# The opening of a fused attention and gated-FFN block: constants ahead of x, statistics of one row pair on ScalarE, packed K norms, and a score bound added by products for the first two score groups

## The chip, the cores and the metric

The kernel runs on one core of a Trainium2 chip. The core has TensorE (PE in the profile, with PEld for its weight loads), VectorE (DVE), ScalarE (ACT), GpSimd (POOL), SyncE (SP) and 16 DMA engines. SP issues nearly all DMAs here. Each engine takes its instructions in the order in which the program gives them; instructions of different engines wait for each other through semaphores. The metric is the device time of one execution in microseconds. The kernel before took 963.77 us as the median of 3 runs (963.26 to 965.14).

## What is computed

One pre-norm transformer block on 2048 rows of 512 values (bf16), with 32 heads of 16 and a hidden width of 1792, without masks, biases or learnt norm weights.

```python
x = A_x
h = x + _A_ref(_layernorm(x, axis=-1), A_wqkv, A_wo)
h2 = h + _B_ref(_layernorm(h, axis=-1), B_w_gate, B_w_up, B_w_down)
# _A_ref: qkv = x @ wqkv; p = softmax(q k^T * Dh**-0.5); o = p v; o @ wo
# _B_ref: (sigmoid(x w_gate) * (x w_up)) @ w_down
```

The softmax runs over all 2048 keys, so 32 x 2048 x 2048 exponentials are taken. B_x is not used.

## The kernel before

**The exponential sets the shape.** Scores are made transposed: a tile is 128 keys by 512 queries of one head. Three such tiles make a group (`groups`, GU = 3), one group is one step, and there are 683 steps. `emit_scores` (L764) issues a step: three products of K (`KT`) with Q (`QB`) into one of two PSUM buffers of three banks (`pss2`, L767), and one ScalarE exponential over 128 x 1536 (L794). In every fourth step from step 8 on, and in some more later (`split`), ScalarE takes two of the three tiles and VectorE the third, in five instructions spread over four steps: L813 from PSUM, L816 and L819 one step on, L822 two steps on and L826 three steps on.

**The softmax bound.** In place of a row maximum the kernel subtracts a bound, the product of the norm of q with the largest norm of a key, and the subtraction is part of the score product. K and Q rows stand at the even partitions of `KT` and `QB`. The odd partitions of `KT` hold 1.0, and those of `QB` hold zero, but for one in each half of 64, which holds the bound. `emit_q_rows` (L215) loads Q into `QB` by four DMAs, `emit_q_bound` (L226) the bound by two; for step 0 the second of these goes out from ScalarE's queue. The bound of a query is `y0` (a root by bit arithmetic of its squared norm, `q_root`) times `nks` (from the largest squared key norm, `k_bound`, L179), rounded into `bnd` (`q_bound`, L203).

**Prologue (L238 to L390), up to step 0.** Eight loads of two row tiles each bring x on SP's queue (L80), three loads the K, Q and V parts of `wqkv` on ScalarE's queue (L82). GpSimd makes the identity and fills `QB[0]`, `KT[:,1]` and the ones column of `Vaug`; VectorE clears `ones_blk`, `km2`, `quad`, fills `KT[:,0]` and clears `acc`. For a pair u of row tiles, `stats` takes two BN_STATS (L139) and two BN_AGGREGATE (L140) and adds the epsilon (L144) on VectorE, then GpSimd raises to the power -0.5 (L146); `apply` (L150) normalises on VectorE; `trans` transposes on TensorE (L273) and copies on ScalarE (L278). The order is stats of pair u+1, then apply of pair u. Between them come K of head block 0 in four chunks of 512 rows (`k_chunk`, L288, the last by halves), Q of chunk 0, seven V tiles (`v_tile`, L160 and L212), and for each K chunk a norm product over all 128 columns of `ones_blk` (`norm`, L169) and a maximum (`k_max`, L173). `k_bound` and the bound close it. The small constants `head_of` and `ones_blk` are finished behind `stats(0)` (L320, L323). `gate` (L388) is a GpSimd copy that waits for `bnd`; behind it GpSimd clears `QB[1]`, makes `same` (L958), fills `KT[:,2]` to `KT[:,7]` (L433), clears `wo_pad` (L954) and copies `ident_f`.

The prologue has six one-bank PSUM tiles in turn (`pm_tile`), which become the two score buffers; besides there are one bank for `acc` and one for `ps_misc`, which the later fills use (`pmh["pool"]`).

**Steps.** In step i the program emits the scores, then the products with V that are due (`emit_pv`, L857, into `acc`, by `plan_pv`, three key tiles of a head group per four steps), then due callbacks (`later`), then filler products (`emit_fill`, at the rate of `rate(i)`, L755). The filler is one long generator (L742): V tiles 7 to 15 (`fill_v`, L408), K and Q of the other head blocks (`fill_k`, L422, with the fills of `KT` on GpSimd at L433), Q of the later chunks, then for each finished chunk the output projection and the FFN. When a head group of four ends, `emit_norm` (L834) copies `acc` to `xs_all` (L838), sends the sums through DRAM (`sd`), takes the reciprocal five steps later (L849), sends it through DRAM again (`rd`) to `rb_all`, and scales ten steps later (L845). `QB` of the next head group is loaded at key tile 12 of the present one in chunks of 512 queries, and at key tile pair 0 in the two last chunks of 256.

Of the kernel before, what the change touches and what calls it, by code (L numbers as in the profile page):

```python
# [10 lines left out]
FP32 = mybir.dt.float32  # L11
BF16 = mybir.dt.bfloat16
# [6 lines left out]
def kernel(  # L19
# [30 lines left out]
    GM = 188  # L50
    G1 = 680
    QS = DH ** -0.5 * 1.4426950408889634 * 2.0 ** 23
    LEAD = 0.106445681
    PA, PB, PC = 0.70747575 / LEAD, 1.37730748 / LEAD, 1.77561468 / LEAD
    ONE_BITS = (127.0 + math.log2(LEAD)) * 2.0 ** 23
# [23 lines left out]
    for i in range(8):  # L79
        nc.sync.dma_start(out=xb[:, 2 * i:2 * i + 2, :], in_=x_v[:, 2 * i:2 * i + 2, :])  # L80
    for part in (1, 0, 2):
        nc.scalar.dma_start(out=wqkv_sb[:, :, part * D:(part + 1) * D],  # L82
                            in_=wqkv_v[:, :, part * D:(part + 1) * D])
# [24 lines left out]
    nks = const.tile([P, 1], FP32)  # L108
    bnd = const.tile([P, QC], BF16)
# [62 lines left out]
    def k_max(ps, n):  # L172
        nc.vector.tensor_reduce(out=km2[:, n:n + 1], in_=ps[:], axis=AX.X, op=ALU.max)  # L173
# [5 lines left out]
    def k_bound():  # L179
        m2 = small.tile([P, 1], FP32, name="m2")  # L180
        nc.vector.tensor_reduce(out=m2[:], in_=km2[:], axis=AX.X, op=ALU.max)
        z0 = small.tile([P, 1], mybir.dt.int32, name="z0")
        sqrt_bits(z0[:], m2[:])
        z = z0[:].bitcast(FP32)
        ri = small.tile([P, 1], FP32, name="ri")
        nc.vector.reciprocal(out=ri[:], in_=z)
        tq = small.tile([P, 1], FP32, name="tq")
        nc.vector.scalar_tensor_tensor(out=tq[:], in0=ri[:], scalar=m2[:, 0:1], in1=z,
                                       op0=ALU.mult, op1=ALU.add)
        nc.vector.tensor_scalar(out=nks[:], in0=tq[:], scalar1=-0.5175, scalar2=None, op0=ALU.mult)  # L190
# [45 lines left out]
    NV0 = 7  # L236

    def prologue(pro):  # L238
        warm = pro.tile([P, 8], FP32, name="warm")
        nc.vector.memset(warm[:], 0.0)  # L240
        nc.scalar.activation(out=warm[:], in_=warm[:], func=ACT.Exp)
        make_identity(nc, ident_bf[:])
        nc.gpsimd.memset(pw_neg[:], -0.5)
        nc.gpsimd.memset(QB[0][:], 0.0)
        nc.gpsimd.memset(KT[:, 1, :], 1.0)
        nc.gpsimd.memset(Vaug[:, :, :, DH:DH + 1], 1.0)
# [5 lines left out]
        nc.vector.memset(KT[:, 0, :], 1.0)  # L252
        nc.vector.memset(acc[:], 0.0)

        mvs, rss, xns, pts, sqs, pns = {}, {}, {}, {}, {}, {}
        ku = stages[0]

        def stats(u):
            mvs[u] = pro.tile([P, 2, nc.vector.BN_AGGR_DIM], FP32, name="mvs", bufs=3)
            for i in range(2):  # L260
                ln_stats(xb[:, 2 * u + i, :], mvs[u][:, i, :])
            rss[u] = ln_rstd(mvs[u], 2)

        def apply(u):
            xns[u] = pro.tile([P, 2, D], BF16, name="xn2", bufs=3)
            for i in range(2):
                ln_apply(xns[u][:, i, :], xb[:, 2 * u + i, :], mvs[u][:, i, :], rss[u][:, i:i + 1])

        def trans_mm(u):
# [5 lines left out]

        def trans(u):
            trans_mm(u)
            nc.scalar.copy(out=xnT[:, :, 2 * u * P:(2 * u + 2) * P], in_=pts[u])  # L278

        def square(key, ps, scale=1.0):  # L280
            sqs[key] = pro.tile([P, QC], BF16, name="sq", bufs=3)
            nc.scalar.activation(out=sqs[key][:], in_=ps[:], func=ACT.Square, scale=scale)

        def norm(key):
            pns[key] = pm_tile()
            norm_mm(pns[key], 0, sqs[key][:])

        def k_chunk(n):  # L288
            ps = pm_tile()
            for c in range(DC):  # L290
                qk_mm(ps, 1, 0, n, c)
            cols = slice(n * QC, (n + 1) * QC)
            nc.scalar.copy(out=ku[:, cols], in_=ps[:])
            square(n, ps)
            k_spread(ku, 0, cols, nc.sync)

        def k_half(ps, u):
            hc = slice(QC // 2 * (u % 2), QC // 2 * (u % 2 + 1))
            for c in range(DC):
                nc.tensor.matmul(ps[:, hc], lhsT=wqkv_sb[:, c, D:D + P], rhs=xnT[:, c, u * QC // 2:(u + 1) * QC // 2],  # L300
                                 start=(c == 0), stop=(c == DC - 1))

        def q_chunk():
# [4 lines left out]
            square("q", ps, QS)  # L308
            ready.add(("q", 0, 0))
            emit_q_rows(0)  # L310

        def v_tile(t, copy=nc.scalar.copy):
            ps = pm_tile()
            for c in range(DC):
                v_mm(ps, t, c)
            v_store(t, ps, copy)
            ready.add(("v", t))

        def consts():
            nc.vector.tensor_reduce(out=head_of[:], in_=ident_bf[:].rearrange("p (h r) -> p h r", r=DH),  # L320
                                    axis=AX.X, op=ALU.max)
            for b in range(4):
                nc.vector.tensor_copy(out=ones_blk[:, b, :, 8 * b:8 * b + 8],  # L323
                                      in_=head_of[:].unsqueeze(1).to_broadcast([P, 4, 8]))

        def ln_step(u):
            if u + 1 < NT // 2:
                stats(u + 1)
            apply(u)

        stats(0)
        consts()
        ln_step(0)
        trans(0)
        ln_step(1)
        trans(1)
        v_tile(0)
        ln_step(2)
        trans(2)
        k_chunk(0)  # L340
        ln_step(3)
        trans(3)
        q_chunk()
        norm(0)
        ln_step(4)
        trans(4)
        k_chunk(1)
        norm("q")
        ln_step(5)
        trans(5)  # L350
        v_tile(1)
        v_tile(2)
        norm(1)
        ln_step(6)
        trans(6)
        ps2 = pm_tile()
# [655 lines left out]
```

## Time and profile before

| | before |
|---|---|
| median of 3 runs | 963.77 us (963.26 to 965.14) |
| time of the profiled execution | 962.96 us |
| its span, first to last instruction | 961.1 us |
| TensorE, VectorE, ScalarE, GpSimd busy | 826.7, 788.1, 895.3, 41.5 us |
| first exponential starts | 34.24 us |
| last exponential (step 682) starts | 929.73 us |
| DMA moved | 28.38 MB |

Times in a profile count from the first instruction of the profiled execution, in us; a mean duration is in ns. A row of the instruction groups gives line, engine, operation, tile written and tiles read, the shapes and how often it ran, then busy time and mean duration, then the engine's idle time in front of it and who ended most of it. The chain of waits is followed back from the last instruction: a row gives start, length and what the chain spent it on; "DMA" there is from issue to landing, "issue" is time in which the engine waited for nothing that the profile shows.

### The profile page before, as it was taken

How to read it: one execution, taken by the hardware profiler on the slowest of the kernel's cores; microseconds unless marked ns; L12 is line 12 of the kernel's file. 1: busy time of each engine (PE TensorE's matmuls, PEld its weight loads, DVE VectorE, ACT ScalarE, POOL GpSimd, SP SyncE). 2: the span in 40 equal slices, each digit the busy share in tenths (PEclk: the TensorE clock that was granted, in tenths of full speed). 3: DMA queues.
4: the chain of work that ended last, by engine and by line, in shares of the span. 5: the costliest groups of instructions: out<-in, count | busy, mean ns of one | idle time of the engine just before them, and what ended most of it. 6: DMA issues, size and time to landing. Idle time of an engine off the chain costs nothing.

```text
span 961.1 us, 17150 instructions
## 1 busy us (share of the span) xinstructions
PE 826.7 (86%) x6327; PEld 337.8 (35%) x6425; DVE 788.1 (82%) x1428; ACT 895.3 (93%) x767; POOL 41.5 (4%) x49
## 2 busy tenths in 40 slices
PE   4887888888788999988788999988788999888998
PEld 2322222222222332222222233222355555455646
DVE  8589998888788888899888888888888788777653
ACT  4789999999999999999999999999998999899872
POOL 4700000000000000000000000000000000000000
PEclk9999999999999999999999999999999999999999
DMA  5001350000013000000011000001011000110010
GB/s 160 21 8 50 114 117 17 16 16 2 16 26 103 16 16 17 19 12 26 14 27 26 16 16 15 14 15 26 16 31 23 16 13 13 27 32 16 9 35 12
DMA packets 37500, 28.38 MB, mean 30 GB/s; under 512 B 17708, under 2 KB 32776, under 8 KB 37416
## 3 DMA queue, kind: packets, MB, share of 16 engines
q1 hardware_dynamic: 35828, 25.71, 10.4%
q10 hardware_dynamic: 1588, 1.58, 0.5%
q8 instruction: 50, 0.82, 0.4%
q14 instruction: 34, 0.28, 0.1%
HBM read 20.31 MB, written 2.61 MB: 24 GB/s over the span
## 4 chain that ended last, share of the span: by engine, by line
PE 40%; DVE 26%; ACT 23%; issue 7%; DMA 3%; SPq 1%; ACTq 0%; DVEq 0%; POOL 0%; POOLq 0%
PE pss L783 20%; ACT pt L794 12%; PE acc L864 8%; PE pm L530 6%; ACT stg L794 4%; ACT wd L794 4%; DVE stg L813 3%; ACT QTu L794 2%; PE pm L546 2%; DVE reg L816 2%; DVE st L139 2%; DVE pt L826 2%; DVE y L822 2%; PE pm L506 2%; DVE reg L543 1%
## 5 line engine op out<-in xcount | busy, mean ns | idle before, releaser
L783 PE MATMUL pss<-QB,KT 64*128 64x512 bf16 (+3 forms) x2542 | 475.8, 336 | 86.9 <-ACT pt L794 43.8
L794 ACT ACTIVATE pt<-pss 128x1536 bf16<-128x1536 f32 (+1 forms) x392 | 501.1, 1363 | 16.3 <-PE pss L783 12.0
L783 PEld LDWEIGHTS <-KT 64*128 64x128 bf16 (+1 forms) x2560 | 181.4, 95 | 345.3 <-issue 232.5
L794 ACT ACTIVATE stg<-pss 128x1536 bf16<-128x1536 f32 (+1 forms) x140 | 183.1, 1355 | 4.6 <-PE pss L783 3.8
L813 DVE TENSOR_SCALAR stg<-pss 128x512 int32<-128x512 f32 x123 | 84.8, 689 | 69.3 <-PE pss L783 53.0
L864 PE MATMUL acc<-pt,Vaug 128*17 128x512 bf16 (+1 forms) x1471 | 112.5, 338 | 4.5 <-DVE xs_all L838 3.2
L794 ACT ACTIVATE wd<-pss 128x1536 bf16<-128x1536 f32 (+1 forms) x80 | 103.8, 1390 | 2.7 <-PE pss L783 2.4
L794 ACT ACTIVATE QTu<-pss 128x1024 bf16<-128x1024 f32 (+1 forms) x71 | 95.5, 1345 | 1.7 <-PE pss L783 1.2
L819 DVE SCALAR_TENSOR_TENSOR y<-reg 128x512 f32<-128x512 f32 x123 | 85.2, 692 | 4.2
L822 DVE SCALAR_TENSOR_TENSOR y<-y,reg 128x512 f32<-128x512 f32 x123 | 84.2, 684 | 1.1
L864 PEld LDWEIGHTS <-Vaug 128*17 128x17 bf16 x2560 | 50.4, 89 | 96.1 <-issue 80.8
L530 PE MATMUL pm<-reg,reg 128*128 128x512 bf16 (+1 forms) x252 | 55.6, 333 | 8.7 <-DVE reg L543 6.6
L530 PE MATMUL pm<-reg,wu 128*128 128x512 bf16 (+1 forms) x280 | 58.1, 338 | 1.5 <-ACT sg L535 1.2
L546 PE MATMUL pm<-wd,reg 128*128 128x512 bf16 x173 | 51.2, 381 | 5.7 <-issue 2.9
L146 POOL TENSOR_TENSOR rs<-ve,pw_neg 128x1 f32<-128x1 f32 (+1 forms) x24 | 17.7, 736 | 888.9 <-DVE ve L144 758.0
L816 DVE TENSOR_SCALAR reg<-stg 128x512 int32<-128x512 int32 x123 | 52.0, 423 | 2.0
L864 PE MATMUL acc<-stg,Vaug 128*17 128x256 bf16 (+1 forms) x564 | 50.6, 326 | 0.6 <-DVE stg L826 0.4
L543 DVE SCALAR_TENSOR_TENSOR reg<-sg,pm 128x512 bf16<-128x512 f32 x56 | 38.2, 682 | 13.9 <-PE pm L530 13.5
L826 DVE SCALAR_TENSOR_TENSOR pt<-y,stg 128x512 bf16<-128x512 f32 x70 | 47.8, 683 | 1.8
L535 ACT ACTIVATE sg<-pm 128x512 f32<-128x512 f32 x56 | 35.6, 637 | 10.1 <-PE pm L530 9.8
L813 DVE TENSOR_SCALAR wd<-pss 128x512 int32<-128x512 f32 x45 | 30.9, 688 | 15.9 <-PE pss L783 14.9
L165 PE MATMUL pm<-reg 128*128 128x512 bf16 x112 | 35.6, 391 | 2.2 <-issue 0.8
(129 smaller groups left out, 707.5 us busy)
## 6 DMA issues: line engine op xcount, KB each, us to landing
rb_all<-rd SPq DMA_DIRECT2D x96, 64.0 KB
reg<-in_A_x_dram SPq DMA_DIRECT2D x8, 256.0 KB
xr<-in_A_x_dram SPq DMA_DIRECT2D x16, 128.0 KB
out_dram<-ob SPq DMA_DIRECT2D x15, 128.0 KB
rb_all<-rd SPq DMA_DIRECT2D x60, 32.0 KB
KT<-stg SPq DMA_DIRECT2D x7, 256.0 KB
reg<-in_B_w_gate_dram SPq DMA_DIRECT2D x4, 448.0 KB
wu<-in_B_w_up_dram SPq DMA_DIRECT2D x4, 448.0 KB
```

Of the source, the lines that this page charges most:

```text
L165: nc.tensor.matmul(ps[:], lhsT=wqkv_sb[:, c, w0:w0 + P], rhs=xnT[:, c, n * QC:(n + 1) * QC], start=(c == 0), stop=(c == DC - 1))
L530: nc.tensor.matmul(ps[:, i * w:(i + 1) * w], lhsT=wt[:, c, f * P:(f + 1) * P], rhs=hnT[:, c, 0:w], start=(c == 0), stop=(c == DC - 1))
L543: nc.vector.scalar_tensor_tensor(out=out, in0=a, scalar=1.0, in1=b, op0=ALU.add, op1=ALU.mult)
L546: nc.tensor.matmul(ps[:], lhsT=hT[:, f, tt * P:(tt + 1) * P], rhs=wd[:, f, :], start=(f == 0), stop=(f == FC - 1))
L783: nc.tensor.matmul(pss[:, ui, h * w:(h + 1) * w], lhsT=KT[rows, g, kt * P:(kt + 1) * P], rhs=QB[n_qg % 2][rows, j, 0:w], start=True, stop= ...
L794: ex = nc.scalar.activation(out=pt[:, 0:na, :], in_=pss[:, 0:na, :], func=ACT.Exp, scale=DH ** -0.5 / QS)
L813: return nc.vector.tensor_scalar(out=e_bits, in0=src, scalar1=ONE_BITS, scalar2=0.0, op0=ALU.add, op1=ALU.max)
L816: nc.vector.tensor_scalar(out=e_man, in0=e_bits, scalar1=0x7FFFFF, scalar2=-0x40800000, op0=ALU.bitwise_and, op1=ALU.bitwise_or)
L819: nc.vector.scalar_tensor_tensor(out=e_pol, in0=m, scalar=PA, in1=m, op0=ALU.add, op1=ALU.mult)
L822: nc.vector.scalar_tensor_tensor(out=e_pol, in0=e_pol, scalar=PB, in1=e_man.bitcast(FP32), op0=ALU.add, op1=ALU.mult)
L826: nc.vector.scalar_tensor_tensor(out=dst, in0=e_pol, scalar=PC, in1=e_bits.bitcast(FP32), op0=ALU.add, op1=ALU.mult)
L864: nc.tensor.matmul(acc[32 * j:32 * j + VW, 0:w], lhsT=Vaug[:, kt, 4 * g + j, :], rhs=p[:, h * w:(h + 1) * w], start=(kt == 0), stop=(kt == ...
```

## The change

**Loads.** The first x pair is split: row tile 0 on SP's queue, row tile 1 on ScalarE's. The `wqkv` parts move to SP's queue behind x.

**Constants.** `head_of` and `ones_blk` are made before x arrives; `same` and the ones column of `Vaug` are made on ScalarE; the clear of `acc` moves to the fills. Fills of `KT` and `QB` on GpSimd go over the same bytes as half as many 4-byte elements (two bf16 ones in one word). `gate` now waits for `ones_blk`, and stands in front of the fill of `KT[:,0]` and the clear of `QB[1]`; nothing holds GpSimd behind the last statistics.

**Statistics.** The epsilon add moves from VectorE to GpSimd. Pair 1's mean and variance come from ScalarE: two Identity passes with a sum, two Square passes with a bias and a sum. `stats` runs two pairs ahead of `apply`.

**Norms.** K chunks 0 to 2 put their norms into 32 rows each of one PSUM tile, with one maximum over 96 rows, spread by a small product; chunk 3 goes by halves of 256. `k_bound` drops a Newton step (three of five small instructions) and a slack factor of 1.0735 takes its place; for block 0 the bound comes straight from `z0`.

**First two groups.** `QB[1]` gets a copy of the first Q rows without a bound. Steps 0 and 1 multiply over all 128 rows of it, and add the bound by a second product into the same bank, of a broadcast identity column with `bnd`.

**V.** Three V tiles instead of seven stand ahead of step 0's exponential (the third between the two products of step 0); tiles 3 to 6 go to the filler, 3 and 5 of them through `acc`.

**Steady part.** Next `QB` load at key tile 2 instead of 12 from head group 6 on (`EARLY`); reciprocal and scaling two steps later except for the last head group or two of a chunk (`wait`); where a head group's first key tile is due, the filler comes before the product with V (`early_fill`).

The diff, cut to its core:

```diff
-    for i in range(8):
+    nc.sync.dma_start(out=xb[:, 0, :], in_=x_v[:, 0, :])
+    nc.scalar.dma_start(out=xb[:, 1, :], in_=x_v[:, 1, :])
+    for i in range(1, 8):
         nc.sync.dma_start(out=xb[:, 2 * i:2 * i + 2, :], in_=x_v[:, 2 * i:2 * i + 2, :])
     for part in (1, 0, 2):
-        nc.scalar.dma_start(out=wqkv_sb[:, :, part * D:(part + 1) * D],
+        nc.sync.dma_start(out=wqkv_sb[:, :, part * D:(part + 1) * D],
...
+    def k_fold(kd, n, col):
+        pc = ps_misc.tile([P, 512], FP32, name="pm")
+        nc.tensor.matmul(pc[:, 0:4], lhsT=same[0:n].rearrange("p r h -> p (r h)"), rhs=kd[0:n, :],
+                         start=True, stop=True)
+        k_max(pc[:, 0:4], km2[:, col:col + 1])
...
-    NV0 = 7
+    NV0 = 3
+    OB = 2
+    def fill_ones(eng, ap):
+        eng.memset(ap.bitcast(FP32), TWO_ONES)
...
+        gate = pro.tile([P, 1], BF16, name="gate")
+        nc.gpsimd.tensor_copy(out=gate[:], in_=ones_blk[:, 3, 3, 31:32])
+        fill_ones(nc.gpsimd, KT[:, 0, :])
+        clear(QB[1][:])
...
+        x_sums = sums_act(1)
         stats(0)
-        consts()
-        ln_step(0)
+        stats_act(1, x_sums)
+        stats(2)
+        apply(0)
         trans(0)
-        ln_step(1)
+        stats(3)
+        clear(QB[0][:, 0:2, :])
+        apply(1)
         trans(1)
-        v_tile(0)
-        ln_step(2)
+        apply(2)
         trans(2)
         k_chunk(0)
...
+        v0 = v_prod(0, pm_tile())
+        v_cast(0, v0)
+        stats(7)
+        nc.gpsimd.memset(bnd[:].bitcast(FP32), 0.0)
+        apply(6)
+        norm_part_of(1)
         trans(6)
...
+        q_root(acc, 0)
+        apply(7)
+        v1 = v_prod(1, pm_tile())
+        norm_part_of(2)
+        km4 = small.tile([P, 1], FP32, name="km4")
+        k_max(pnp[0:96, :], km4)
...
+        kd = k_spots(km4, 96)
         ps3 = pm_tile()
         k_half(ps3, 6)
         k_half(ps3, 7)
+        pn3 = pm_tile()
+        norm_half(pn3, 6)
+        k_max(pn3[:, 0:QC // 2], km2[:, 1:2])
+        k_fold(kd, 96, 0)
+        v_cast(1, v1)
+        k_copy(2, ps2)
+        k_copy(3, ps3)
+        pn3 = ps_misc.tile([P, 512], FP32, name="pm")
+        norm_half(pn3, 7)
+        k_max(pn3[:, 0:QC // 2], km2[:, 2:3])
+        m2 = k_most()
+        sqrt_bits(z0[:], m2[:])
+        nc.vector.tensor_scalar(out=bnd[0:32, :], in0=y0[0:32, :].bitcast(FP32), scalar1=z0[0:32, :].bitcast(FP32),
+                                scalar2=-SQRT_SLACK, op0=ALU.mult, op1=ALU.mult)
...
+        emit_q_bound(0)
         k_spread(ku, 1, slice(0, S), nc.sync)
-        gate = pro.tile([32, 1], BF16, name="gate")
-        nc.gpsimd.tensor_copy(out=gate[:], in_=bnd[0:32, 0:1])
-        nc.gpsimd.memset(QB[1][:], 0.0)
...
-            rates = (4.0 if i > 5 else 0.0, 4.0 if i < 6 else 2.0 if i > 16 else 0.0, 0.0, 4.0)
+            rates = (4.0, 4.0 if i < 6 else 2.0 if i > 16 else 0.0, 4.0 if i < 6 else 0.0, 4.0)
...
-        pss = pss2[(i + 1) % 2]
+        pss = pss2[i % 2]
...
+        if i < OB:
+            for ui, (c, g, k, j) in enumerate(group):
+                nc.tensor.matmul(pss[:, ui, :], lhsT=KT[:, g, k * P:(k + 1) * P], rhs=QB[1][:, j, :],
+                                 start=True, stop=False)
+            if i == 0:
+                v_cast(2, v_prod(2, pm_tile()))
+            for ui, (c, g, k, j) in enumerate(group):
+                nc.tensor.matmul(pss[:, ui, :], lhsT=ident_bf[:, j:j + 1].to_broadcast([P, P]), rhs=bnd[:],
+                                 start=False, stop=True)
+            parts = []
...
-            if k == (12 if per_bank(c) == 1 else 0) and j == 3 and n_qg + 1 < len(qgs):
+            if k == (0 if per_bank(c) > 1 else 2 if n_qg in EARLY else 12) and j == 3 and n_qg + 1 < len(qgs):
...
+        wait = 2 if g < NG - 1 - (c == NC - 1) else 0
...
-            later(i + 10, scale)
-        later(i + 5, recip)
+            later(i + 10 + wait, scale)
+        later(i + 5 + wait, recip)
...
+            early_fill = i >= 2 * CYC and any(u[2] == 0 for u in us)
+            for u in us:
+                if early_fill and u[2] == 0:
+                    emit_fill(i)
                 emit_pv(*u[:3], i)
```

## The prediction

> **What bounds it now.** I read the shares first, then ScalarE's busy time by stages, then the chain of waits of the first 60 us, then the rows around ScalarE's later pauses. By the shares ScalarE does most:
>
> ```profile
> PE 826.7 (86%) x6327; PEld 337.8 (35%) x6425; DVE 788.1 (82%) x1428; ACT 895.3 (93%) x767; POOL 41.5 (4%) x49
> ...
> 34.24:100.00 65.76, 61.06 (x49) 1.00 0.09 23
> 100.00:200.00 100.00, 99.86 (x82) 1.00 0.25 63
> ...
> 600.00:700.00 100.00, 97.18 (x82) 1.00 0.07 17
> 700.00:800.00 100.00, 96.46 (x85) 1.00 0.09 21
> 800.00:900.00 100.00, 92.73 (x80) 1.00 0.09 22
> ```
>
> The columns after the stage are its length, ScalarE's busy time, the clock and the DMA. From the first exponential on ScalarE is the bound, so time comes from two places: exponentials that start earlier, and ScalarE's pauses, 4.7 us before 100 and some 15 us behind 300. The way to the first exponential, from the chain of waits (start, length, what):
>
> ```profile
> 0.74 3.74 DMA reg<-in_A_x_dram
> ...
> 9.96 0.61 DVE st L139
> 10.58 0.02 issue
> 10.60 0.18 DVE mvs L140
> 10.79 0.59 DVE st L139
> 11.37 0.02 issue
> 11.40 0.19 DVE mvs L140
> 11.59 0.02 issue
> 11.61 0.17 DVE ve L144
> 11.78 0.64 DVE xn L150 x2
> ...
> 30.82 0.48 DVE bnd L203
> ...
> 31.37 1.99 DMA QB<-bnd
> 33.36 0.12 issue
> 33.48 0.60 PE pss L783 x3
> ```
>
> VectorE holds the chain from 4.50 to 25.74: 2.46 us a pair (9.96 to 12.42), of which 1.62 are statistics, 0.19 the epsilon, 0.65 the normalising. Then come transposes, the last K chunk, norms, maxima and bound to 31.30, 2 us of DMA, and the first exponential at 34.24.
>
> **The prologue, step by step.** *Start.* x's first landing, at 4.48, shares the DMA engines with the weights; split and with the weights behind it I take 3.5 (bounds 3.0 and 4.48). The constants (0.73 for `head_of`, 0.41 for four copies) then end at about 2.8, ahead of x; today they lie on the chain. *VectorE* takes seven statistics of 1.62, eight normalisings of 0.65 and `q_root` at 0.60: 3.5 + 11.3 + 5.2 + 0.6, and 0.2 of waiting for GpSimd in front of the first normalising, 20.9 at the end of `apply(7)` against 25.74. *ScalarE* gains four passes of about 0.6 (as a 512-wide Square, 0.62; sums out of an instruction are in no row, 0 to 0.3 each), 0.6 for V's ones and 1.1 for `same`; it stood idle for 6.88 us ahead of its first copy. Pair 1's root is ready at 8.3, wanted at 9.2: if the cover goes, each 0.3 costs its own length. *GpSimd* gets the epsilon adds, 0.2 each beside 0.73 for a root; statistics run two pairs ahead, which hides both. *Weights* behind x: 2.6 MB of x and K at the 263 GB/s of the first 10 us land at about 11 to 12; K's first product needs them at 11.8; 0 to 0.2. On SP's queue three weight issues and four more `QB` issues (0.5 to 0.6 each, 22.6 at the latest today) stand ahead of K copies that nothing needs before step 3: nothing.
>
> Here VectorE is no longer last; **TensorE and ScalarE are**. After `apply(6)` at 19.6 come the transposes, K chunk 2 and V tile 1 (0.86 each), norm product and transposes to 22.7 on TensorE; VectorE's maximum waits for the norm (22.4 to 23.0) and the copy behind it ends at 23.4; K's last half 24.1, its Square 24.5, its norm product behind the fold (free at 24.7) 25.0, maximum 25.5, two small ones 25.8, bound 26.3. V tile 2 stands ahead of the bound's products (three at 0.22 and 0.16 to drain), so these end at 27.4, and so starts the first exponential. If TensorE's pace (0.427 us a 512-wide product until 17.3, 0.216 after) changes at 12.5 or at 18 instead of my 14.7, it is 27.0 or 28.5. *Bound rows by DMA* are now wanted by step 2: today they are there 2.1 us after the bound, now both go through SP behind two K copies, one issue (0.70) later, about 3.6 behind the bound, and step 2 wants its exponential 3.8 behind it with 0.7 of products ahead of that: 0.5 late at worst, 0.3 taken. 0.3 more for hand-overs that I left out: **28.0 in effect, 6.2 earlier**.
>
> **A queue that opens: GpSimd.** Today `gate` holds eight fills (six of `KT`, two of `wo_pad`, 1.745 us apart) until 31.36. After the change nothing does: behind the last root, at 20.2, they run in one piece, six at half the elements, 0.87 (by bytes 1.75), and two at 1.745, to 29.0. What they do to VectorE the trace shows twice. The epsilon add at 6.24 took 0.81 instead of 0.17, to the end of a fill; and in the rows of VectorE (start, length, engine, line, operation):
>
> ```profile
> 46.60 2.25 DVE L816 TENSOR_SCALAR reg<-wd 128x512 int32<-128x512 int32 x1
> ...
> 53.42 0.42 DVE L816 TENSOR_SCALAR reg<-wd 128x512 int32<-128x512 int32 x1
> ```
>
> The long one ran to the end of the last fill, past one boundary between two. So a scaling of 4-byte words in SBUF waits; `bnd` (4-byte in, 0.47) is one, and `apply` (bf16, 0.406) may be. For `apply` the rows speak against it: beside it GpSimd's roots keep 0.72 to 0.79. For `bnd` it costs nothing to a boundary's wait of 0.3 (27.7), or 2.9 if it waits to 29.0; I take the short one.
>
> The Trainium skill, SBUF — State Buffer, section Who interferes with whom, says that VectorE in a two-port mode and GpSimd take a shared port pair as an exclusive lock, and that copies and scalings in SBUF, bf16 ones too, can take it. By that `apply(7)` would wait as well, the third rival below; the trace agrees for 4-byte words (2.25 against 0.42) and not for `apply` beside the roots (0.72 to 0.79).
>
> **The first steps.** V tiles 3 to 6 come after the first exponential now: 0.86 of TensorE and 0.69 of VectorE each. In steps 1 to 5 a step with a V tile takes TensorE 0.6 + 0.86 = 1.47 against 1.34 of exponential; five such steps lag 0.65, and 0.74 is in hand. Later steps hold as many filler products as before, other ones. I take +0.4 (to +2.0 if two tiles show in full). Against it the 2.25 of L816, which is on the chain and ends in a ScalarE pause of 1.78 at 53.41, goes: the fills are over 9 us before. -1.7, together **-1.3**. Half as many bound instructions on VectorE, the other fills and the swapped score buffers: nothing, beside ScalarE's 99%.
>
> **The steady part.** The delayed reciprocal meets the one pause that is plainly its own (chain, start, length):
>
> ```profile
> 829.95 3.23 DMA s_all<-sd
> 833.19 0.02 issue
> 833.21 0.20 DVE r_all L849
> ```
>
> VectorE waited there, its next FFN output came late, TensorE waited 1.78 and ScalarE 1.95. Two steps, 2.7 us, cover it. The other three such waits (535, 746, 877) lie beside ScalarE's work or cost under 0.8. The filler ahead of a new head group covers only one product (0.2 to 0.3) of TensorE's waits for `xs_all` (0.95 at 645 and 728). Earlier `QB` loads are six issues moved on SP; no product behind step 2 waits for `QB` today, so they gain nothing but can meet another DMA. I take **-1.9** (bounds -4, with the pauses of 1.0 at 647 and 1.3 at 730, and +1, if the shifted transfers meet others).
>
> **Sum.** -6.2 - 1.3 - 1.9 = -9.4. The profiled execution took 962.96 (its span 961.1 and 1.9 around it), so 953.6; the median of the runs lies 0.8 above it, so 954.4.
>
> **Rivals**, each in the median's terms.
> - *The bound waits for the last fill.* For: L816 let one boundary pass. Against: that was 0.1 us behind its issue. 29.0 + 0.5 + 0.8 of products gives 30.3, 2.9 later than 27.4, less 0.3 as step 2's rows are then no later: 957.0. Chance 0.24.
> - *The V tiles eat it.* Steps 9 to 29 already pause for 4.7 us, so two tiles show in full and steady changes give nothing: -6.2 + 1.5 + 0 = -4.7: 959.0. Chance 0.14.
> - *`apply(7)` waits for the fills too.* Then it ends at 29.7 and the rest of its chain, 5 us, gives 34.7: +0.5 - 1.3 - 1.9: 961.1. Chance 0.11.
> - *Slower: the same wait, with long fills.* If a fill of 4-byte words goes by bytes, 1.75, six of them end at 35.0 and the first exponential starts at 40.7: +6.5 - 3.2: 967.1. It decides from 1.56 us a fill on. Against: the small fills go by elements (128 in 0.205, 2048 in 1.8). Chance 0.05.
>
> The forecast has 0.46; its own range, from the bounds above, is 950.5 to 960. About 0.2% is what a measurement of this kernel can tell from no change; of the third rival, which lies across that line, half counts as the same. Faster 0.89, same 0.06, slower 0.05. The range 950.5 to 960.5 leaves out the last two rivals.
>
> **What would show it.** First exponential near 28; `apply(7)` ending near 21; GpSimd's fills ending near 29 at 0.87 each; `bnd` at about 0.5 and not 2 or more; L816 at 0.42 throughout; no pause of 1 us or more in steps 9 to 29 or near step 617. It is wrong if `apply` or `bnd` shows microseconds, if step 2 waits for `QB` by over 0.6, or if pauses behind step 300 add to more than today's 15 us.

## The result, and the profile after

The changed kernel took 973.84 us (median of 4 runs, 973.56 to 976.31), the kernel before 964.45 in the same comparison: ratio 1.0103, 95% interval 1.0081 to 1.0126. It is 9.4 us slower where 9.4 us faster was forecast. The profiled execution took 976.31 (span 974.5); it is the slowest of the four, while the profiled execution of before (962.96) lies below its four. So the two profiles lie 13.4 apart where the medians lie 9.4 apart, and the places below add to more than the loss of the medians. From the page of the profile after:

```profile
PE 839.3 (86%) x6334; PEld 339.5 (35%) x6433; DVE 786.2 (81%) x1410; ACT 900.3 (92%) x779; POOL 34.6 (4%) x57
...
PEclk9799999999999999999999999999999999999989
```

ScalarE is still the bound. It does 5.0 us more work (900.3 against 895.3), of which 4.9 lie ahead of the first exponential (21.82 against 16.92 before); behind that the work is the same, and what is lost there is idle time. New are the digits below 9 in TensorE's clock, at the beginning and in the tail. The start of each exponential, set against its counterpart before, says where the time went (after minus before, us):

| exponential of step | 0 | 8 | 13 | 36 | 40 | 380 | 385 | 535 | 541 | 682 | end of span |
|---|---|---|---|---|---|---|---|---|---|---|---|
| after | +3.3 | +4.4 | +3.2 | +3.7 | +6.3 | +5.9 | +9.1 | +7.6 | +9.5 | +8.3 | +13.4 |

Five losses stand out: the first exponential (37.58 instead of 34.24), steps 36 to 40, 380 to 385, 535 to 541, and the tail behind the last exponential.

**The first exponential.** GpSimd's order in the profile after (start, length, line, operation, in brackets its idle time and what ended it):

```profile
18.95 0.53 POOL L256 MEMSET KT<- 128x512 f32 x1 [1.32 <-DMA KT<-stg]
...
25.39 0.53 POOL L256 MEMSET KT<- 128x512 f32 x1 [4.91 <-DMA KT<-stg]
...
37.98 0.95 POOL L256 MEMSET KT<- 128x1024 f32 x1 [10.83 <-DMA KT<-stg]
```

These three fills of later parts of `KT` wait for transfers that write other, earlier parts, the K copies. The first two stand ahead of the roots of pairs 6 and 7 in GpSimd's order, so these roots wait too. Pair 6's still comes in time (it ends at 20.48, and VectorE takes up `apply(6)` at 21.14 without a pause); pair 7's does not. The chain of waits goes through exactly this (start, length, what):

```profile
23.41 1.92 DMA KT<-stg
...
25.39 0.53 POOL KT L256
...
26.19 0.72 POOL rs L292
...
26.93 0.42 DVE xn L328
```

`apply(7)` starts at 26.93; the forecast had it end at 20.9. TensorE has nothing to do meanwhile (idle for 3.04 us up to 27.40) and pays a second time. By stages of the profile after (length, TensorE's busy time, weight loads, VectorE, ScalarE, GpSimd; then clock and DMA):

```profile
24.00:27.40 3.40, 0.36 (x2) 0.06 (x2) 0.47 (x2) 0.00 (x0) 1.68 (x4) 0.94 0.09 23
27.40:37.60 10.20, 7.90 (x30) 3.94 (x32) 3.10 (x11) 3.42 (x8) 0.00 (x0) 0.52 0.18 41
```

In the first stage TensorE works 0.36 us of 3.40; in the next its clock is half (from 27.02 to 37.26), and three 512-wide score products take 1.44 us of the chain (32.99) instead of the 0.65 that the next three take (37.40). Behind that the clock is full.

**The delayed reciprocal.** The second loss of weight is on SP's queue. Near step 372 in the profile of before (start, length of all issues, queue, line):

```profile
510.73 1.71 SPq L853 DMA_DIRECT2D rb_all<-rd  x4
512.49 1.45 SPq L511 DMA_DIRECT2D xr<-in_A_x_dram  x1
```

and VectorE's residual sum that reads this row:

```profile
517.02 0.68 DVE L515 TENSOR_TENSOR reg<-pm,xr 128x512 f32<-128x512 f32 x1
```

The chain of the profile after, at the same steps:

```profile
517.11 2.73 DMA rd<-r_all
...
521.61 2.23 DMA xr<-in_A_x_dram
...
523.93 0.70 DVE reg L591
```

Both kernels issue the x rows (`xr`) behind the reciprocal's transfers. Before, the row went out at 512.49 and the residual sum came at 517.02 without a wait. Now the reciprocal is late, `rb_all` waits for `rd` on SP, the rows behind it are late too, and the residual sum (L591) waits for them (1.24 here, and 2.30 for the sum at 733.90, within steps 535 to 541); the transposes behind it keep TensorE idle for 1.68 us, and its clock halves from 528.78 to 532.19. In the tail the same order costs more (chain of the profile after):

```profile
938.13 3.42 DMA rb_all<-rd
...
941.63 0.43 DVE OT L932
```

Head group 5's delayed transfers stand ahead of group 6's sums (`sd`): these go out from 930.99, 2.9 behind the copy that makes them (928.10), where before it was 0.45 (920.28 and 919.83). Group 6's reciprocal runs at 935.21 instead of 924.55 in before, and the last scaling ends 4.1 us behind the last exponential's start (942.06 to 938.00). Before, it ended with it (929.90 to 929.73). TensorE idles and runs at half clock from 941.79 to 948.62.

**Steps 36 to 40.** Of the profile after, VectorE and then GpSimd:

```profile
85.25 0.24 DVE L936 RECIPROCAL r_all<-s_all 128x16 f32<-128x16 f32 x1
85.41 2.09 DVE L902 TENSOR_SCALAR reg<-wd 128x512 int32<-128x512 int32 x1
```

```profile
85.42 3.83 POOL L1041 MEMSET wo_pad<- 128x2048 bf16 x2
```

The held fills have moved here (two of `KT` start at 83.63, after 43.81 of waiting, with two of `wo_pad` behind them). The delayed reciprocal pushes L902 (normally 0.42) to the moment at which a fill of `wo_pad` begins, and it takes 2.09. TensorE is short of work again and its clock halves from 91.88 to 95.29.

### The profile page after: what moved, and what is told of

Read it like the earlier page. It is cut to its first block, busy times and chain, and to the rows that moved or that the text cites. A ratio compares the mean times of both kernels' runs of the same rounds, so it can differ in the third digit from the quotient of the medians.

```text
span 974.5 us, 17192 instructions
## 1 busy us (share of the span) xinstructions
PE 839.3 (86%) x6334; PEld 339.5 (35%) x6433; DVE 786.2 (81%) x1410; ACT 900.3 (92%) x779; POOL 34.6 (4%) x57
## 4 chain that ended last, share of the span: by engine, by line
PE 42%; ACT 24%; DVE 22%; issue 7%; DMA 3%; SPq 1%; POOL 0%; ACTq 0%; DVEq 0%
PE pss L869 20%; ACT pt L880 13%; PE acc L951 8%; PE pm L606 6%; ACT stg L880 4%; ACT wd L880 4%; DVE stg L899 3%; PE pm L622 2%; ACT QTu L880 2%; DVE y L908 2%; PE pm L582 2%; DVE st L146 1%; DVE reg L902 1%; DVE pt L912 1%; DVE reg L619 1%
## 5 line engine op out<-in xcount | busy, mean ns | idle before, releaser
L869 PEld LDWEIGHTS <-KT 64*128 64x128 bf16 (+1 forms) x2554 | 179.1, 95 | 344.7 <-issue 232.7
L902 DVE TENSOR_SCALAR reg<-stg 128x512 int32<-128x512 int32 x123 | 51.5, 418 | 2.1
L619 DVE SCALAR_TENSOR_TENSOR reg<-sg,pm 128x512 bf16<-128x512 f32 x56 | 38.4, 685 | 15.1 <-PE pm L606 14.7
L153 POOL TENSOR_TENSOR rs<-ve,pw_neg 128x1 f32<-128x1 f32 x16 | 12.0, 753 | 821.6 <-DVE ve L151 811.6
```

What stands on the lines that cost most here:

```text
L619: nc.vector.scalar_tensor_tensor(out=out, in0=a, scalar=1.0, in1=b, op0=ALU.add, op1=ALU.mult)
L869: nc.tensor.matmul(pss[:, ui, h * w:(h + 1) * w], lhsT=KT[rows, g, kt * P:(kt + 1) * P], rhs=QB[n_qg % 2][rows, j, 0:w], start=True, stop= ...
L902: nc.vector.tensor_scalar(out=e_man, in0=e_bits, scalar1=0x7FFFFF, scalar2=-0x40800000, op0=ALU.bitwise_and, op1=ALU.bitwise_or)
```

## The experiments

Two theories stood against each other. The first: the prologue is late only because the fills hold the roots, and the delay of two steps loses the rest. The rival: the prologue's new order, or the other edits of the steady part, lose by themselves. Each comparison ran beside the kernel before (medians 964.1 to 964.5).

**e1: fill K[1] early.** Both fills of `KT[:,1]` right behind that of `KT[:,0]`.

```diff
         fill_ones(nc.gpsimd, KT[:, 0, :])
+        fill_ones(nc.gpsimd, KT[:, 1, :])
...
-        fill_ones(nc.gpsimd, KT[:, 1, 0:S // 2])
...
-        fill_ones(nc.gpsimd, KT[:, 1, S // 2:S])
```

> The changed kernel with both fills of KT[:,1] moved up on GpSimd, right behind the fill of KT[:,0], before any DMA into KT is out. Nothing else is changed. Theory (a fill of KT through a 4-byte view waits for the K copies' DMA into another part of KT, and the roots of pairs 6 and 7 stand behind it on GpSimd): no root waits, apply(7) ends near 21 instead of 27.7, TensorE has no 3 us pause and its clock stays up, the first exponential starts at 28 to 30 instead of 37.6, the kernel takes 964 to 966 instead of 973.8. The loss of 3 us in steps 34 to 40 stays. Rival (the roots wait for something else, or TensorE is last anyway): first exponential stays above 35, time above 971.

Measured: 969.66 (964.68 to 974.1), ratio 1.0067 (1.0042 to 1.0091). `apply(7)` ends at 22.87, the first exponential starts at 30.92, 6.7 earlier than in after. The loss at 36 to 40 is still there. The held root is the cause of the late start. The time is 4.2 below after and not the 8 to 10 that were expected: the six runs spread over 9.4 us, with mean clocks from 0.986 to 0.996.

**e2: no delay.** After, with `wait = 0`.

```diff
-        wait = 2 if g < NG - 1 - (c == NC - 1) else 0
+        wait = 0
```

> The changed kernel with wait = 0 throughout: reciprocal and scaling at 5 and 10 steps as in the kernel before. Theory (in the last chunk the delayed reciprocal of head group 5 puts five DMAs in front of the sums of group 6 on SP, so the last scaling comes 3.9 us late and TensorE's clock drops): last scaling at about the last exponential's start and not 3.6 behind it, 4 to 5 us less from there to the end, 969 to 970. The pause of 1.95 near step 617 comes back, so at best 969, and 971 if that takes 2. Rival (the tail's loss comes from the clock alone, by the place of its window): no change, 973 to 974.5.

Measured: 963.56 (961.6 to 968.26), ratio 1.0000 (0.9985 to 1.0016): 10.3 below after, more than was expected (3 to 5). The losses at 36 to 40, at 380 to 385 (+0.2), at 535 to 541 and in the tail are gone. The rival falls: of the steady part it is the delay that loses.

**e3: late Q loads, and e4: filler behind the product with V.** Two other edits of the steady part undone, each alone, from after.

```diff
-    EARLY = range(6, 64)
+    EARLY = range(0)
```

```diff
-            early_fill = i >= 2 * CYC and any(u[2] == 0 for u in us)
+            early_fill = False
```

> The changed kernel with the next QB load at key tile 12 in every head group, as before. Theory (earlier QB loads free no product and hold nothing): within 1 us of the changed kernel, 973 to 975. Rival (the six issues moved on SP are what made the x rows late near 521 and 736): 2 to 4 us less, 970 to 972.

> The changed kernel with the filler behind the product with V everywhere, as before. Theory (the order covers 0.2 to 0.3 us at each of 39 head groups, and few of them are late): 0 to 2 us more, 974 to 976. Rival (the product with V comes later by the filler and delays the scores behind it): 1 to 3 us less.

Measured: e3 973.99 (ratio 1.0102, 1.0089 to 1.0115), e4 976.96 (ratio 1.0129, 1.0114 to 1.0144). The early Q loads do nothing that shows. Without the filler ahead of a new head group the kernel with the delay takes 3.1 us more; the intervals of e3 and e4 just touch.

**e5: e1 and e2 together**, both diffs above.

> Both: the fills of KT[:,1] early and wait = 0. Theory (the held roots and the delayed reciprocal are separate losses): first exponential near 30.9 as with the fills alone, no pause of TensorE for the clock to drop in, last scaling at the last exponential's start, 958 to 961. Whether the loss of 3 us at steps 36 to 40 stays tells if it hangs on the delayed reciprocal (gone: 958) or on GpSimd's fills there (stays: 961). Rival (without the delay the kernel with held roots was at 963.6 only because the clock's windows fell well; then nothing is left to win): 962 to 964.

Measured: 957.92 (956.68 to 958.99), ratio 0.9933 (0.9917 to 0.9948), faster than both kernels. First exponential 30.83. Against before, exponential 40 stands at -3.1, 300 at -3.6, 682 at -4.9: nothing is lost on the way.

**e9: the delay alone, on the kernel before.**

```diff
+        wait = 2 if g < NG - 1 - (c == NC - 1) else 0
...
-            later(i + 10, scale)
-        later(i + 5, recip)
+            later(i + 10 + wait, scale)
+        later(i + 5 + wait, recip)
```

> The kernel before with the delay of reciprocal and scaling alone, nothing of the prologue. Theory (the last chunk's delayed DMAs stand in front of the next head group's sums on SP): last scaling 3 to 4 us behind the last exponential's start, 2 to 5 us more than before, 966 to 969, though the pause of 1.95 near step 617 goes. Rival (the delay is harmless by itself, the tail's loss needs the changed prologue or a fallen clock): 962 to 964.

Measured: 972.21 (970.1 to 976.66), ratio 1.0089 (1.0064 to 1.0114), more than was expected. So the delay loses by itself, 7.9 us over the 964.27 beside it, at the same places (steps 380 to 385 +4.9, 535 to 541 +4.0, tail +3.8, in the profile of its slowest run). SP's queue and the residual sum in its profile:

```profile
518.73 0.42 SPq L511 DMA_DIRECT2D xr<-in_A_x_dram  x1
```

```profile
521.00 0.69 DVE L515 TENSOR_TENSOR reg<-pm,xr 128x512 f32<-128x512 f32 x1 [1.96 <-DMA xr<-in_A_x_dram]
```

The row goes out 6.2 us later than in before (518.73 against 512.49), 2.4 of which the kernel had lost by step 380, and the sum that did not wait now waits 1.96.

**e6: K as eight tiles instead of one, and e7: that with no delay, V's ones on VectorE, and V tile 2 behind the bound's products.** Both from after.

```diff
-    KT = const.tile([P, NG, S], BF16)
+    class Heads:
+        def __init__(self):
+            self.of = [const.tile([P, S], BF16, name=f"KT{g}") for g in range(NG)]
...
+    KT = Heads()
```

and in e7 also

```diff
-        nc.scalar.copy(out=Vaug[:, :, :, DH:DH + 1],
-                       in_=warm[:, 0:1].to_broadcast([P, NT * H]).rearrange("p (t h o) -> p t h o", h=H, o=1))
...
+        nc.vector.memset(Vaug[:, :, :, DH:DH + 1], 1.0)
...
-                v_cast(2, v_prod(2, pm_tile()))
...
+                v_store(2, v_prod(2, pm_tile()), nc.vector.tensor_copy)
+                ready.add(("v", 2))
...
+        wait = 0
```

> The changed kernel with KT as eight separate tiles of one head group each, every instruction in its old place. Theory (the waits of the KT fills come from the 4-byte view of one large tile, whose other parts the K copies are written to): no fill waits for a DMA, roots 6 and 7 come at once, first exponential near 31; the six later fills and the two of wo_pad run right behind the last root, from 22.4 to about 31.6, so the bound multiply at 28.2 meets them: nothing more if the fills are in 4-byte words and it gets in between two, up to 1.8 if it meets a wo_pad fill, 3.4 if it waits for all. No loss at steps 36 to 40, since the fills are over. 966 to 969, the late tail included. Rival (the waits are real ones, for other data in the same rows): fills wait as before, first exponential 35 to 38, time 973 to 975.

> KT as eight tiles, wait = 0, V's ones column filled on VectorE ahead of x instead of in 2.35 us on ScalarE, V tile 2 behind the bound's products and copied by VectorE. Theory: mean of pair 1 at 5.7 instead of 7.5, so the first root 1.8 earlier, bound's products not behind V tile 2 (0.9): first exponential at 28 to 29, if the bound multiply is not held by fills, 30 if it is; everything after as in the kernel before or better by 1.3 at step 13: 956 to 958. Rival (TensorE's cold pace sets the prologue whatever ScalarE does): first exponential above 30, 959 to 961.

Measured: e6 967.37 (ratio 1.0028, 1.0016 to 1.0041), e7 959.37 (ratio 0.9950, 0.9935 to 0.9965), in the range that its expectation gave to the rival. With separate tiles no fill waits for a K copy: the waits in after come from the one tile. Then the fills run where the prediction had put them, and meet VectorE. Of e7, the first four fills on GpSimd (two of `wo_pad` follow from 24.85, two more of `KT` from 28.36), and then VectorE:

```profile
21.00 3.90 POOL L263 MEMSET KT<- 128x1024 f32 x4
```

```profile
20.83 3.18 DVE L334 TENSOR_SCALAR xn<-reg,mvs,rs 128x512 bf16<-128x512 bf16 x2
...
24.86 1.81 DVE L191 TENSOR_SCALAR kd<-quad,km 96x4 bf16<-96x4 bf16 x1
...
28.39 1.19 DVE L459 TENSOR_SCALAR bnd<-y,z 32x512 bf16<-32x512 f32 x1
```

The two instructions of `apply(7)` take 3.18 together (0.73 in e5), `kd` 1.81 (0.21 in e5), `bnd` 1.19 (0.47 in e5). Each ends soon after the end of a fill, the first of the two of `apply(7)` after the second fill that it meets; so a waiting instruction gets in between two fills and does not wait for the last one. The first exponential of e7 came at 31.25, after a drop of the clock at 29.04. Where the root is free and the other fills are held (e5, `apply(7)` ending at 22.89 against 24.01 here), the waits that the change had by accident keep the fills away from its prologue.

The Trainium skill, SBUF — State Buffer, section Who interferes with whom, says that VectorE in a two-port mode, which scalings in SBUF can enter, and GpSimd exclude each other for a whole instruction. These rows agree with it (3.18 against 0.73 for two bf16 scalings). The rows that the prediction set against it, `apply` beside the small roots, did not decide it, and why no wait shows in them stays open.

**e10: e5 with the two edits of V from e7**, K in one tile.

> The kernel with KT[:,1] filled early and no delay (957.92), with two more edits: V's ones column by a VectorE fill ahead of the first statistics instead of the 2.35 us write on ScalarE, and V tile 2 behind the first tile's bound products, with its copy on VectorE. The later fills stay one tile, so they stay held behind the K copies' transfer, away from the prologue. Theory: ScalarE's first statistics start about 1.9 us earlier and the V tile's 1.0 us leaves the path; the chain apply(0) to apply(7) moves by 1.3 (as where the heads' K were eight tiles: apply(7) began at 20.83 against 22.15), and the first exponential comes at 28.2 to 29.0 instead of 30.83. Time 955.3 to 956.5. Rival: the K copies' transfer then ends in time to let the fills go ahead of the bound's multiply; that is held as with eight tiles (1.19 instead of 0.47), and the time stays at 957 to 958.

Measured: 957.37 (955.65 to 960.06), ratio 0.9927 (0.9910 to 0.9944), not to be told from e5, and above the 955.3 to 956.5 that were expected. `bnd` starts 0.54 earlier (27.57 against 28.11) and is not held, but in the profiled run the clock halved from 27.32 to 30.73 and from 518.84 to 522.25, and by step 6 it stood 0.9 behind e5. The six runs show what the clock does: 955.65 and 955.7 us at a mean granted clock of 1.000, 957.08 and 957.67 at 0.998, 959.63 and 960.06 at 0.996.

**How the delay loses: e11 to e15.** All with early fills; e11 and e12 from e1, with the delay. e11 sends the reciprocal's transfers from GpSimd's queue, e12 leaves the last chunk undelayed:

```diff
-            nc.sync.dma_start(out=rd[:].rearrange("j (a b) -> (j a) b", b=b), in_=r32)
+            nc.gpsimd.dma_start(out=rd[:].rearrange("j (a b) -> (j a) b", b=b), in_=r32)
...
-                nc.sync.dma_start(out=rb[32 * j:32 * j + 32, :], in_=rd[j:j + 1, :].to_broadcast([32, w]))
+                nc.gpsimd.dma_start(out=rb[32 * j:32 * j + 32, :], in_=rd[j:j + 1, :].to_broadcast([32, w]))
```

```diff
+        wait = 2 if g < NG - 1 and c < NC - 1 else 0
```

> The kernel with KT[:,1] filled early and the delay kept (969.66), with one edit: the reciprocal's round trip (rd, and the four rb_all transfers) is issued by GpSimd's queue instead of SyncE's. Theory (the delay costs because these transfers, when late, stand on SyncE's queue ahead of the next chunk's x rows and of the next group's sums): the x rows go out near 512 again, the losses at steps 380 to 385 and 535 to 541 and half or more of the tail's +5 go, and the time is 958 to 961. Rival (the late scaling itself holds the output products, whichever queue carries the reciprocal): 967 to 970 as before. A GpSimd queue that takes longer to issue would show as a later rb_all landing and could add 1 to 2 us in the tail under either.

> The kernel with KT[:,1] filled early (969.66), with the delay of two steps in all query chunks but the last. Theory (the delay loses twice: some 5 us at the chunks' ends, steps 380 to 385 and 535 to 541, and some 4 us in the tail, where group 5's late transfers stand ahead of group 6's sums): only the tail's part comes back, 964.5 to 966.5. Rival (the tail is late only since all is late): 969 to 970.

Measured: e11 985.78 (ratio 1.0214, 1.0191 to 1.0236), a miss. It does take the loss at 380 to 385 down to 0.5 and that at 535 to 541 away, but it loses 18 us between steps 40 and 200, where VectorE waits for `rb_all`. From the list of who waited for that tile (us, times), of e11:

```profile
  DVE OT L931: 34.7, 18
```

VectorE's scalings waited 34.7 us in 18 places, against 6.8 in 4 with SP's queue (e1). So it doesn't tell the theories apart.

e12: 965.39 (964.67 to 968.87), ratio 1.0014 (1.0004 to 1.0025), 4.3 below e1; behind the last exponential it loses nothing against before. The tail's share is 4.3 by the medians, known to some 2.5 us because of the spread of e1; in e1's profiled run, its fastest, the tail loses 1.9. e12 takes the whole delay out of the last chunk, so that the order on SP's queue is what costs there is read from the chain of after and not tried by itself.

**e13** (from e12) asked for the first two x rows of a chunk ahead of time, right behind head group 6's sums.

```diff
-            xr = x_load(t)
+            xr = ahead.pop(t, None) or x_load(t)
...
+        if g == NG - 2 and c < NC - 1:
+            ahead.update((t, x_load(t)) for t in tiles_of(c)[:2])
```

> The kernel of e12 (K[1]'s tiles filled early, the delay in all query chunks but the last; 965.39), with one edit: the x rows of the next output tiles are requested right behind head group 6's sums, so ahead of the delayed reciprocals' transfers on SyncE's queue. Theory (the delay costs at steps 380 to 385 and 535 to 541 because these rows stand behind the late transfers, the residual sum waits for them, TensorE waits 1.2 to 1.7 for its transposes and loses its clock): VectorE's residual sum at 517 no longer waits (0.74 in e12), the two losses of 2.1 each go, and the time is 961 to 963. Rival (the late scaling itself, or VectorE's moved work, holds the output products): the waits for the transposes stay and so does 965.

Measured: 965.21 (963.75 to 970.93), ratio 1.0010 (0.9997 to 1.0023). No effect, and no test either: the row that waits is a later one, and its wait was still there (1.25 at 524.02). **e14** (from e12) requests the rows a tile or two ahead; **e15** is the control, the same in e5.

```diff
-        for tt, t in enumerate(tiles_of(c)):
-            xr = x_load(t)
+        ts = tiles_of(c)
+        xrs = [x_load(t) for t in ts[:2]]
+        for tt, t in enumerate(ts):
+            xr = xrs[tt]
...
             hn = wo_ln(ps, xr, tt)
+            xrs.extend(x_load(t) for t in ts[tt + 2:tt + 3])
```

> The kernel of e12 (K[1]'s tiles early, the delay in all query chunks but the last; 965.39) with the x rows requested a tile ahead: a chunk's first two at once, each further one right after the residual sum two tiles before it, some 15 us ahead of the late transfers (e13 had moved only the first two rows of a chunk, and the row that waits is the fourth). Theory (the delay costs at steps 380 to 385 and 535 to 541 because these rows stand behind the late transfers): no residual sum waits for its row (3.5 us in three places in e12), the losses of 2.1 at each of the two places shrink to 0.5 or less, and the time is 961 to 963. Rival (VectorE's moved work itself makes the residual sum late, or the late scaling holds the output products): the waits for the transposes stay, 964 to 966.

> The control: the same early request of the x rows in the kernel without the delay (957.92), whose residual sums waited for no row. Theory and rival alike: 957 to 958.5. A gain here would mean that the rows' place on the queue is worth something by itself, and e14 would have to be read against it.

Measured: e14 960.74 (958.85 to 962.3), ratio 0.9961 (0.9947 to 0.9976), 4.65 below e12; e15 958.77, ratio 0.9939 (0.9927 to 0.9952), whose interval overlaps that of e5. In e12 three residual sums waited 3.5 us in all for their rows, in e14 none did, and both losses went: 380 to 385 from +2.8 to +0.4, 535 to 541 from +1.9 to -0.3. The theory holds for these two places: there the reciprocal's delay costs through the rows that stand behind its transfers.

What is left of the delay is 2.0 us of e14 over e15. The traces differ most at steps 36 to 44, where e14 loses 4.6 against before and e15 nothing, by the collision with the fills; that it is the whole rest was not tried alone. In e15 the scaling starts 0.14 ahead of the fill (the fill starts at 80.42) and is free:

```profile
80.28 0.47 DVE L907 TENSOR_SCALAR reg<-wd 128x512 int32<-128x512 int32 x1
```

In e14 the delayed reciprocal (0.24 at 80.21) pushes it 0.03 behind the fill (80.37 against 80.34):

```profile
80.37 2.05 DVE L907 TENSOR_SCALAR reg<-wd 128x512 int32<-128x512 int32 x1
```

## Why the prediction was wrong

**The sum, as it came out.** By medians, along the way from before over e5 and e2 to after: -6.4 for the rest of the change (e5 against 964.27), +5.6 for the held roots (e2 over e5), +10.3 for the delay (after over e2). The forecast had -9.4, of which the steady part, mostly the delay, was to give -1.9.

**The step that failed: "Two steps, 2.7 us, cover it … I take -1.9".** Its mechanism was wrong, and so was its upper bound of +1 "if the shifted transfers meet others". The prediction looked at who waits for the reciprocal, and not at what stands behind its transfers on SP's queue: five issues, of which four wait for the first one's landing. On the kernel with early fills the delay costs 11.7 (e1 over e5): 4.3 in the tail (e1 to e12), 4.65 through the x rows (e12 to e14), and some 2.8 that are left (e14 over e5; 2.0 over its control e15), for which the trace shows the collision at steps 36 to 40. The first two shares hang on single medians, the first on the wide one of e1. Nor was there much to win: between steps 600 and 617, where the pause was to be covered, after gains 0.8 on before, but e2, without the delay, gains 0.6 there too.

**"After the change nothing does"** (holds GpSimd) failed as well. The step counted GpSimd's fills as work without inputs. They wait for transfers into another part of the same tile, and with separate tiles they don't (e6). In before the bf16 fills of the same tile show no such wait: all are done by 48.6, though four of them stand in the program behind K copies that go out at 70.19 and 70.83. That the 4-byte view of the tile makes the difference is argued from this, and was not tried alone. The prediction did not ask what stands behind a fill in GpSimd's order: two roots.

**A fall of the clock was in no term.** The prediction allowed for the time at which TensorE's pace first rises (12.5 or 18 instead of 14.7), not for a clock that falls again. In the prologue alone, after and e2 show what that costs. Both have `apply(7)` at 26.93 and TensorE idle for 3.04; in after the clock then fell and the first exponential came at 37.58, in e2 it did not and it came at 34.33. The two kernels have the same prologue, so its order alone does not decide which.

**Point by point.**
- *x at 3.5*: right (3.48). *V's ones at 0.6*: no row of before showed this term for ScalarE, and GpSimd's fill of the same 512 places took 2.26 there (at 4.77), against 1.81 for 2048 elements in a row. It took 2.35 (below). ScalarE's first statistics start at 6.10, and the small product of their sums (`nm`, at 7.53) stands on GpSimd ahead of pair 0's epsilon add (7.85) and root (8.15), so `apply(0)` comes at 8.92 instead of 6.9. In e10, with the column on VectorE, `apply(7)` comes 0.9 earlier and the first exponential of the profiled run 0.15.
- *First exponential 28.0*: 30.83 in e5, where the roots are free, so -3.4 and not -6.2. The chain is the forecast one, `apply(7)` ending 2.0 late and the bound 2.3 late.
- *First steps*: the 2.25 of L816 went as forecast (L902, its counterpart, takes 0.42 at 51.13 and 56.65 in after, though 2.09 later, at 85.41); in e5 this gives -1.2 between steps 8 and 13 (forecast -1.7), and the V tiles cost +1.1 up to step 8 (forecast +0.4, bound 2.0). Together -0.1 instead of -1.3. From step 13 to 682 e5 gains another 1.4, which no term had; what gives it was not tried.
- *The filler ahead of a head group*: forecast at next to nothing, worth 3.1 beside the delay (e4). *Early Q loads*: nothing, as forecast (e3).
- *Rivals*: the burst of fills did not meet the bound or `apply(7)` in after, because the fills were held. Where they were let go (e6, e7) `apply(7)` did wait, so the prediction gave this rival too little weight; but the wait is from fill to fill and not, as the rival had it, to the last one. The slower rival, long fills, was not it: a 4-byte fill of 1024 took 0.95.
- *What would show it* named a right sign, "if pauses behind step 300 add to more than today's 15 us": from step 300 to 682 after loses another 2.5 against before, and 5.1 behind that.

## What to carry to other kernels

Before a callback with DMAs is moved in time, list what is issued behind them on the same queue and when that is wanted: a later transfer moves everything behind it, and a queue that waits for its own first transfer holds all the rest. Where one engine serves fills and a short link of a critical chain, put the fills where nothing stands behind them, and look whether parts of one tile are tracked as one. A short wait of TensorE can cost more than its length, since the products behind it may run at half clock; leave room for that in the range.

## What was not expected of the hardware

- TensorE's granted clock in the records was half or full, and the stretches at half clock are multiples of 3.413 us: 27.02 to 37.26, 91.88 to 95.29, 528.78 to 532.19, 941.79 to 948.62 in after. In the 3.413 us ahead of these drops TensorE was busy for 22%, 40%, 33% and 41%. On this grid of 3.413 us, all 16 windows at full clock in which TensorE was busy for less than 44% were followed by half clock, over the sixteen profiles; none over 63% was, and between the two the clock sometimes fell and mostly did not (worked out from the rows of TensorE's products, a few of which can be missing). The Trainium skill, TensorE: Matmul & The Clock Gate, section What's actually happening, says that the window is 3413 ns and free-running. The trace agrees, and the place of the window within the run fits with how one kernel's times spread with the mean clock (e10 above). In e2 the same idle 3.04 us lay across two windows (22.84 to 26.25, busy 45%, and 26.25 to 29.66, busy 51%), and the clock stayed; in after they lay mostly in one (23.61 to 27.02, 22%).
- A ScalarE copy that spreads one column over 512 separate 2-byte places of each partition took 2.35 us; a 512-wide Identity pass took 0.63, and reading its sum another 0.19. From the profile after:

```profile
2.71 2.35 ACT L265 CAST Vaug<-warm 128x512 bf16<-128x512 f32 x1
...
6.10 0.63 ACT L307 ACTIVATE sq<-reg 128x512 bf16<-128x512 bf16 x1
```

- The same VectorE scaling took 0.47 us when it started 0.14 ahead of a GpSimd fill (e15) and 2.05 when it started 0.03 behind one (e14).
- Short transfers requested from GpSimd's queue came late for VectorE in 18 of 39 places (34.7 us in e11). In 20 of the 39 the profile puts the end of GpSimd's idle time before `rd` down to VectorE's scaling of 4-byte words. Why they came late was not settled.
